# S5 scan and FFN under one gate: another order of loads and first matmuls, odd inputs seeded in PSUM

## Chip, cores, metric

One NeuronCore of one Trainium2 chip. The metric is device time in microseconds of one execution, the lower the better; for the kernel before, the median of six runs. TensorE is called PE in the profile, VectorE DVE, ScalarE ACT, GpSimd POOL, and SyncE SP; SP and ACT issue all DMAs here.

## What is computed

x has 2048 tokens of 448 columns, in bf16. A gate g weighs two branches: a diagonal complex state space layer (448 states) and an FFN (448 to 1792 to 448, silu between).

```python
g = sigmoid((x * gate_w).sum(-1, keepdims=True))
Lam_bar = exp(dt * Lam);  B_bar = ((Lam_bar - 1) / Lam)[:, None] * (B_re + 1j * B_im)
Bu = x @ B_bar.T
for t in range(L):                  # h is complex, 448 states
    h = Lam_bar * h + Bu[t]
y = 2 * (h @ (C_re + 1j * C_im).T).real + x * Dskip
out = g * y + (1 - g) * (silu(x @ w1) @ w2)
```

## The kernel before

The time axis is cut into pairs of tokens. Row k of `x2` holds tokens 2k (even, columns 0 to 447) and 2k+1 (odd); each of the two streams has 1024 positions, in halves h = 0 and 1 of 512. The scan runs over pairs: its input is Bu(odd) + lambda Bu(even), with lambda = lr + i li, its decay lambda squared; its results are the odd states, and the even ones follow from them.

**Tiles.** 448 = 3 x 128 + 64. Contractions over 448 take three steps j of 128 rows and a remainder of 64. `pair` (353) works on two banks of PSUM at once: each step is two half-row matmuls (64 rows, 512 columns), the lower half into one bank, the upper half into the other; then the remainder; and when the next pair has been started (`settle`, 334), the same main steps with the halves swapped. Of the remainder one half row lies in XT and the other in XR, a copy of 64 rows in the other partition half (`swap_xr`, 237). `late` (363) does the same with the remainder last. States are in blocks pt = 0 to 2 of 128 (real and imaginary parts in tiles m = 2pt and 2pt+1) and pt = 3, whose 64 real and 64 imaginary rows share one tile (its weights are BR, copied from BT in line 612).

**Stages.** FFN1 works on chunks c = 0, 1 (even x, h = 0, 1) and 2, 3 (odd x): 14 blocks fb of 128, silu by ACT from two banks into AT (416). FFN2 (723) makes four 128-token tiles of a chunk, 14 matmuls of 448 columns each. `bu` (757) multiplies x by B for one block and half, even and odd, and ACT copies both to SBUF: even to VE (781), odd to HS (785). `scan` on DVE: `weigh` (809) makes odd + lambda * even in three operations; `turn` rotates by tables COS and SIN and runs the real scan (834), `back` rotates back, `even` (848) makes the even states. `scan3` does pt = 3 and swaps halves by DMA. Then y (935 to 969): a tile's bank is seeded with the scaled FFN result (`yseed`) and gets seven matmuls, five in `yopen` and two (block 2) in `yclose`; `yout` scales and stores it. Block 2's scan is cut in halves and comes last.

**Order.** `Tracker` records instructions per engine in program order and puts a wait where a buffer's last writer or readers ask for it; nothing is reordered. So lines 988 to 1092 are the order written by hand, `run(g, n)` takes n steps of a generator, and `nxt` (319) deals out the eight banks in turn.

**The opening.** 26 warm-up matmuls (446) run while x and W1 load. Even x of half 0 comes as it is (XA0, XA1, XB), TensorE transposes it in blocks (`turn_x`, 450), and DVE copies these from PSUM to XT (`turned_x`, 459). All other transposed x and B come by DMA transposes on SP. `ffn1_first` (394) does steps j = 0 to 2 of six blocks at full row width. Between steps, the rows R (log_dt, Lambda, Dskip) are turned to columns (430) and a chain of small operations on DVE and ACT makes the coefficients (506 to 536); then GpSimd, DVE and ACT make the tables (`phases`, `tables`).

```python
        for j in range(2):
            turn_x(j)
            turned_x(j)
        first = ffn1_first()
        next(first)
        rd()
        T.op("pe", mm_cols, reads=["R0", "R1", "R2", "R3", "Rd", "ID"], writes=["ps7"])
```

## Time and profile before

| | |
|---|---|
| Runs | 138.76 to 139.16 us, median 139.07 (six) |
| The profiled execution | 138.98 us, its span 137.1 us |
| Busy: PE, DVE, ACT, POOL | 132.7, 121.3, 94.7, 21.7 us |
| FFN2 matmuls | 224 of 448 columns, 42.9 us |
| FFN1 half-row matmuls (XT) | 325 of 512 columns, 39.9 us |
| silu on ACT | 28, mean 1019 ns |
| DMA | 12.07 MB, mean 88 GB/s |

The page's span is the time between the first and the last recorded event on the core, the execution's own time is longer. A timeline row reads: start, length, engine, source line, operation, result <- operands, shape, count, and in brackets the idle time before the row with what ended it. Rows of matmuls overlap in their recorded lengths, so that start to start is the pace. A row of groups gives busy time, mean ns of one, and idle time before. A row of waits gives total, times and longest, in us.

### The profile page before, as it was taken

The numbers are of one execution on the slowest core, as the hardware profiler recorded it, in microseconds if no ns is written. First come the engines' busy times: TensorE is split into PE (matmuls) and PEld (weight loads), VectorE is DVE, ScalarE is ACT, GpSimd is POOL, SyncE is SP. The second block draws the span as 40 slices with busy tenths as digits, with TensorE's granted clock in tenths as the row PEclk, the third lists the DMA queues.
The fourth block names the chain that finished last, engine by engine and source line by source line (L and its number), as shares of the span: only waits on it lengthen the run. The fifth ranks groups of instructions, "written<-read, shape, count | busy, mean of one in ns | idle before, by whom it ended". The sixth has DMA issues, their size and how long they took to land.

```text
span 137.1 us, 2412 instructions
## 1 busy us (share of the span) xinstructions
PE 132.7 (97%) x959; PEld 64.9 (47%) x959; DVE 121.3 (88%) x152; ACT 94.7 (69%) x154; POOL 21.7 (16%) x32
## 2 busy tenths in 40 slices
PE   7899999999999999999999999999999999999992
PEld 7344434444434554444554444445555555555561
DVE  1379799969979999999999999999999999999663
ACT  0469799678999999799999159797124337789100
POOL 7105998406910000000000000000000000000000
PEclk9999999999999999999999999999999999999999
DMA  3999378599899220003012000000000000132124
GB/s 101 348 255 275 69 160 169 100 387 361 201 162 114 44 66 0 5 0 77 0 25 51 5 0 0 0 5 0 0 0 0 0 5 33 67 100 67 60 74 134
DMA packets 24641, 12.07 MB, mean 88 GB/s; under 512 B 16628, under 2 KB 24184, under 8 KB 24632
## 3 DMA queue, kind: packets, MB, share of 16 engines
q1 hardware_dynamic: 23044, 10.83, 32.2%
q10 hardware_dynamic: 1588, 1.11, 2.7%
q8 instruction: 7, 0.11, 0.4%
q14 instruction: 2, 0.02, 0.0%
HBM read 5.51 MB, written 1.84 MB: 54 GB/s over the span
## 4 chain that ended last, share of the span: by engine, by line
PE 78%; DVE 7%; ACT 5%; DMA 2%; POOL 2%; issue 2%; SPq 1%; ACTq 0%; DVEq 0%
PE ps L345 32%; PE ps L735 31%; PE ps L939 14%; ACT AT L416 3%; DMA R<-in_A_Lambda_re_dram 2%; ACT CO L686 2%; DVE FP L557 2%; POOL FP L550 1%; SPq L228 1%; POOL G L552 1%; DVE TMPS L963 1%; DVE BT L610 1%; DVE BR L612 1%; DVE P L500 1%; DVE P L497 1%
## 5 line engine op out<-in xcount | busy, mean ns | idle before, releaser
L735 PE MATMUL ps<-W,AT 128*128 128x448 bf16 x224 | 42.9, 353 | 0.0
L345 PE MATMUL ps<-XT,W1E 64*128 64x512 bf16 x325 | 39.9, 376 | 0.0
L735 PEld LDWEIGHTS ps<-W,AT 128*128 128x128 bf16 x224 | 21.7, 98 | 21.2 <-ACT HS L785 0.4
L416 ACT ACTIVATE AT<-ps 128x1024 bf16<-128x1024 f32 x28 | 27.9, 1019 | 4.7 <-PE ps L345 4.5
L345 PEld LDWEIGHTS ps<-XT,W1E 64*128 64x128 bf16 x325 | 16.8, 94 | 19.5 <-DVE IOTA L743 0.5
L345 PE MATMUL ps<-XT,BT 64*128 64x512 bf16 x168 | 19.9, 376 | 0.1
L748 ACT ACTIVATE BT<-ps,GT 128x448 bf16<-128x448 f32 x8 | 5.1, 633 | 13.1 <-PE ps L735 13.1
L345 PEld LDWEIGHTS ps<-XT,BT 64*128 64x128 bf16 x168 | 8.0, 94 | 10.4 <-ACT AT L416 0.6
L939 PE MATMUL ps<-CO,VE 128*128 128x448 bf16 (+1 forms) x63 | 11.6, 332 | 0.0
L939 PE MATMUL ps<-CO,HS 128*128 128x448 bf16 x56 | 11.6, 352 | 0.0
L781 ACT ACTIVATE VE<-ps 128x1024 bf16<-128x1024 f32 (+1 forms) x9 | 7.5, 834 | 5.4 <-PE ps L345 5.4
L834 DVE TENSOR_TENSOR_SCAN G<-P,Q 128x1024 f32<-128x1024 f32 (+1 forms) x6 | 11.2, 1911 | 0.0
L345 PE MATMUL ps<-XR,W1E 64*128 64x512 bf16 x25 | 9.2, 376 | 0.0
L939 PEld LDWEIGHTS ps<-CO,VE 128*128 128x128 bf16 x63 | 6.1, 98 | 4.7
L793 DVE SCALAR_TENSOR_TENSOR HS<-VE,P,G 128x512 bf16<-128x512 bf16 (+1 forms) x10 | 8.1, 856 | 0.2
L939 PEld LDWEIGHTS ps<-CO,HS 128*128 128x128 bf16 x56 | 5.5, 98 | 5.1
L785 ACT ACTIVATE HS<-ps 128x1024 bf16<-128x1024 f32 (+1 forms) x9 | 7.5, 837 | 0.0
L793 DVE SCALAR_TENSOR_TENSOR G<-VE,P,HS 128x1024 f32<-128x1024 bf16 (+1 forms) x5 | 7.5, 1490 | 0.1
L790 DVE TENSOR_TENSOR Q<-G,COS 128x2048 bf16<-128x2048 f32 (+1 forms) x4 | 7.0, 1756 | 0.1
L790 DVE TENSOR_TENSOR Q<-G,SIN 128x2048 bf16<-128x2048 f32 (+1 forms) x4 | 7.0, 1750 | 0.0
L598 DVE TENSOR_TENSOR XN<-XN,DB 128x1792 bf16<-128x1792 bf16 x4 | 4.4, 1090 | 1.3 <-DMA DB<-in_A_Dskip_dram 1.2
L790 DVE TENSOR_TENSOR Q<-Q 128x1024 bf16<-128x1024 bf16 (+1 forms) x9 | 5.2, 573 | 0.3
(118 smaller groups left out, 176.3 us busy)
## 6 DMA issues: line engine op xcount, KB each, us to landing
W<-in_B_w_dram SPq DMA_DIRECT2D x1, 1568.0 KB, 12.3
XN<-in_A_x_dram SPq DMA_DIRECT2D x1, 896.0 KB, 9.8
out_dram<-OT SPq DMA_DIRECT2D x8, 112.0 KB, 1.7
out_dram<-TMPS SPq DMA_DIRECT2D x7, 112.0 KB, 1.7
W1E<-in_B_w_dram SPq DMA_DIRECT2D x3, 224.0 KB, 4.1
HS<-HS SPq DMA_DIRECT2D x4, 128.0 KB, 2.3
W1E<-in_B_w_dram SPq DMA_DIRECT2D x1, 384.0 KB, 5.5
XN<-in_A_x_dram SPq DMA_DIRECT2D x1, 384.0 KB, 6.6
```

What stands on the lines that cost most here:

```text
L345: ins = pe.matmul(ps[:, bank, :], w(p, j), xh(odd, h, j, p), start=start and j == js[0], stop=stop and j == js[-1])
L416: T.op("act", lambda e: e.activation(a[:, fb:fb + n, :], ps[:, bank:bank + n, :], AF.Silu), reads=[f"ps{bank + i}" for i in range(n)], wri ...
L557: T.op("dve", lambda e: e.scalar_tensor_tensor(X, RR, MAGIC, X, ALU.subtract, ALU.subtract), reads=[f"F{pt}", f"G{GP[pt]}"], writes=[f"F{p ...
L598: T.op("dve", lambda e, v=v: e.tensor_tensor(v, v, DB[:, :].unsqueeze(1).to_broadcast([128, 4, D]), ALU.mult), reads=ks + ["DB"], writes=[ ...
L735: ins = pe.matmul(ps[:, bank, 0:D], a[:, fb, q * 128:(q + 1) * 128], W2[:, fb, :], start=(first and fb == 0), stop=(fb == NFB - 1), skip_g ...
L748: T.op("act", lambda e: e.activation(bs(tile), ps[:, bank, 0:D], AF.Copy, scale=sc), reads=[f"ps{bank}", "GT2" if h else "GRI"], writes=ks)
L781: T.op("act", lambda e: e.activation(VE[:, m0:m0 + n, hs], ps[:, b0:b0 + n, :], AF.Copy), reads=pe_, writes=[f"V{m}_{h}" for m in ms])
L785: T.op("act", lambda e: e.activation(HS[:, m0:m0 + n, 8 + h * 512:8 + (h + 1) * 512], ps[:, b1:b1 + n, :], AF.Copy), reads=po_, writes=[f" ...
L790: T.op("dve", lambda e: e.tensor_tensor(o, a, b, op), reads=reads, writes=writes)
L793: T.op("dve", lambda e: e.scalar_tensor_tensor(o, a, s, b, ALU.mult, ALU.add), reads=reads, writes=writes)
L834: T.op("dve", lambda e, c=c, init=init: e.tensor_tensor_scan(G[:, c, w], rb, Q1[:, c, w], init, ALU.mult, ALU.add), reads=[f"Q1{c}", "rr", ...
L939: ins = pe.matmul(ps[:, bank, c], state(kt, odd, m), CO[:, m, c], start=False, stop=(m == YB[-1]), skip_group_check=True)
```

## The change

It changes no arithmetic but that of the weighing in blocks 1 and 2, and adds no pass over data.

- **Loads.** The first x comes in four row blocks and two more column blocks, W1's first 896 columns for j = 0, 1 in two parts, alternately on SP and ACT; the rows R stand after x's first four parts. All of W1 is issued ahead of the first DMA transpose; of these, the second even half of x comes first.
- **Opening.** 22 warm-up matmuls, then two more after four transposes; step j = 0 of `ffn1_first` runs in two halves of 256 columns; transposes and copies are by half for j = 0, 1.
- **Order.** Three remainders first; three pairs of FFN1 on chunk 1 stand ahead of the first `bu`. `skip(n)` leaves out n bank numbers. The scan generators have other steps, so that DVE's order differs too.
- **Seeded odd Bu** for blocks 1 and 2: `bu_even`, then ACT copies the result to VE and writes VE times lr into the two banks into which `bu_odd` adds; `weighed` needs two operations, with an operand in PSUM. Block 2's Bu moves into FFN1 on chunk 2.
- **FFN2 on chunk 0**: no ACT seeds; DVE evacuates all four tiles.
- **XR for odd x**: two DVE copies for a DMA on ACT. `even` of block 1 uses FP instead of G.
- **y**: odd tiles first within each half, the last tile stored in parts of 280 and 168 columns instead of 224 and 224.

```diff
-NWARM = 26
+NWARM = 22
...
+        for k, eng in enumerate(("sp", "act")):
+            ld_x(eng, k)
+        ld_w("sp", 0, 0, FJ, "a")
+        ld_w("act", 0, FJ, FA, "b")
+        for k, eng in ((2, "sp"), (3, "act")):
+            ld_x(eng, k)
+        for i, (eng, v) in enumerate((("sp", A_log_dt), ("sp", A_Lambda_re), ("act", A_Lambda_im), ("act", A_Dskip))):
+            ld_row(eng, i, v)
+        ld_w("sp", 1, 0, FJ, "a")
+        ld_w("act", 1, FJ, FA, "b")
+        for i, eng in enumerate(("sp", "act")):
+            ld(eng, XH[:, 2 * i:2 * i + 2, 256:512], x0[:, 2 * i:2 * i + 2, 256:512], XA[4 + i])
+        ld("sp", W1E[0:64, 3, 0:FA], B_w1[384:448, 0:FA], "W1Ea0")
+        ld_w("act", 2)
+        T.op("act", lambda e: e.activation(JK[:, 0:1], HP[:, :], AF.Exp), reads=["HP"], writes=["JK0"])
...
+        ld_w3("sp", "W1Ee", FB, F_FF)
...
+        ldt(XT[:, 0:3, 512:1024], x2[512:1024, 0:384], "XTe1")
+        ldt(XT[:, 3:4, 512:1024], x2[512:1024, 384:512], "XTer1")
+        for i, src in enumerate((A_B_re, A_B_im)):
+            ldt(BT[:, 0:3, i * D:(i + 1) * D], src[:, 0:384], f"BT{i}")
...
-            for j in range(3):
+            for j, h in ((0, 0), (0, 1), (1, None), (2, None)):
+                c = slice(0, 512) if h is None else slice(256 * h, 256 * h + 256)
...
+                    if (j, h, fb) in ((0, 0, 3), (0, 0, 5), (1, None, 1), (1, None, 3)):
                         yield
...
+        warm(NWARM, 5)
+        PB = (6, 7, 6, 7)
...
         for j in range(2):
-            turn_x(j)
-            turned_x(j)
+            turn_x(j, 0)
+            turned_x(j, 0)
+        warm(2, 5)
         first = ffn1_first()
         next(first)
+        turn_x(0, 1)
+        turned_x(0, 1)
         rd()
+        next(first)
+        turn_x(1, 1)
+        turned_x(1, 1)
+        next(first)
...
-        ld_w3("act", "W1Ee", FB, F_FF)
...
         phases2(0)
+        swap_xr("dve", 1, 0)
         phases2(2)
         phases(3)
+        phases(1, "dve")
         T.op("dve", lambda e: e.tensor_copy(BT[0:64, 3, :], BT[64:128, 3, :]), reads=BTK[2:4],
              writes=["BTz"] + BTK[2:4])
         T.op("dve", lambda e: e.tensor_copy(
             BR[:, :, :].rearrange("p j (c n) -> p j c n", c=2),
             BT[:, :, :].rearrange("p j (c n) -> p j c n", c=2)[:, :, :, 384:448]), reads=BTK, writes=["BR"])
+        swap_xr("dve", 0, 1)
         phases2(3)
-        phases(1, "dve")
         phases2(1)
-        swap_xr("dve", 1, 0)
...
-            first = c != 2 and (c, q) not in ((0, 2), (0, 3))
+            first = c != 2
...
+            if c == 0:
                 T.op("dve", lambda e: e.scalar_tensor_tensor(
...
+        def bu_even(pt, h):
+            m, hs = 2 * pt, slice(h * 512, (h + 1) * 512)
+            b = [nxt(), nxt()]
+            vs = [f"V{m}_{h}", f"V{m + 1}_{h}"]
+
+            def done():
+                o = obank[pt, h] = [nxt(), nxt()]
+                T.op("act", lambda e: e.activation(VE[:, m:m + 2, hs], ps[:, b[0]:b[0] + 2, :], AF.Copy),
+                     reads=[f"ps{i}" for i in b], writes=vs)
+                T.op("act", lambda e: e.activation(ps[:, o[0]:o[0] + 2, :], VE[:, m:m + 2, hs], AF.Copy,
+                                                   scale=c1("lr", pt)), reads=vs + ["lr"], writes=[f"ps{i}" for i in o])
+
+            pair(*[(b[i], 0, h, lambda p, j, i=i: bt(p, j, m + i)) for i in range(2)], BTK[0:2] + XE[h][0],
+                 BTK + XE[h][0] + XE[h][1] + [f"XR{h}a"], done)
+
+        def bu_odd(pt, h):
+            m, o = 2 * pt, obank[pt, h]
+            pair(*[(o[i], 1, h, lambda p, j, i=i: bt(p, j, m + i)) for i in range(2)], BTK[0:2] + XO[h][0],
+                 BTK + XO[h][0] + XO[h][1] + [f"XR{h}b"], lambda: None, seeded=True)
...
+            def weighed(h):
+                w, o = slice(h * 512, (h + 1) * 512), obank[pt, h]
+                stt(u[:, 0, w], ve[:, 1, w], nli, ps[:, o[0], :], lk + [vk[1][h], f"ps{o[0]}"], [uk[0][h]])
+                stt(u[:, 1, w], ve[:, 0, w], li, ps[:, o[1], :], lk + [vk[0][h], f"ps{o[1]}"], [uk[1][h]])
...
-                t = TG if cut else G
-                tgk = ["F1", "CT0", "CT1"] if cut else GK
+                t, tgk = (TG, ["F1", "CT0", "CT1"]) if cut else (G, GK)
+                if pt == 1:
+                    t, tgk = FP[:, 0:2, :], ["F0", "F1", "CT0", "CT1"]
                 stt(t[:, :, :], hp[:, :, w], lr, ve[:, :, w], lk + hk + [f"HSz{pt}"] + v0[0] + v0[1], tgk)
                 stt(ve[:, 0, w], hp[:, 1, w], nli, t[:, 0, :], lk + hk + tgk, he_(a, h0, h1) + v0[0])
                 stt(ve[:, 1, w], hp[:, 0, w], li, t[:, 1, :], lk + hk + tgk, he_(b, h0, h1) + v0[1])
 
+            for h in range(2):
+                if pt:
+                    weighed(h)
+                else:
+                    weigh(h, h + 1)
+                yield
...
-        ffn1_rem(first, 0)
+        def skip(n):
+            for _ in range(n):
+                nxt()
+
+        for fb in (0, 2, 4):
+            ffn1_rem(first, fb)
         pair(*ffn1_pair(0, NF1))
-        ffn1_rem(first, 2)
-        ffn1_rem(first, 4)
-        settle()
-        for i, _ in enumerate(ffn1(0, NF1 + 2)):
-            if i:
-                run(t0, 1)
+        run(ffn1(0, NF1 + 2))
+        late([ffn1_pair(1, 0)])
+        run(t0, 1)
+        for fb in (2, 4):
+            pair(*ffn1_pair(1, fb))
+            run(t0, 1)
         bu(0, 0, late)
-        run(t0)
         bu(3, 0, late)
-        late([ffn1_pair(1, fb) for fb in (0, 2)])
+        pair(*ffn1_pair(1, 6))
         load_w2()
         bu(0, 1, split=True)
         bu(3, 1)
...
+        bu_even(1, 0)
...
+        f = ffn1(1, 8)
...
+        bu_even(1, 1)
-        T.dma("act", lambda e: e.dma_start(XR[0:64, :], XT[64:128, 7, :]), reads=XO[0][3:] + XO[1][3:],
-              writes=["XR0b", "XR1b"])
-        bu(1, 0)
+        bu_odd(1, 0)
+        run(g2, 2)
+        skip(2)
+        run(f)
+        run(g2, 2)
+        bu_odd(1, 1)
         run(g2, 3)
-        bu(1, 1)
...
         run(s0, 1)
+        run(s1, 1)
         run(g3, 1)
-        run(s0, 1)
-        for q in (2, 3):
-            ffn2_seed(q, q, 0)
-        run(t3)
+        run(s1, 1)
         ffn2(0, 0)
...
+        f = ffn1(2)
+        for i in range(4):
+            run(f, 1)
+            if i:
+                run(g2, 1)
+        bu_even(2, 0)
+        run(g2)
+        run(f, 1)
+        run(g3)
+        bu_even(2, 1)
+        run(f, 1)
+        run(t1, 1)
+        bu_odd(2, 0)
+        run(t1, 1)
+        skip(2)
+        run(f)
+        bu_odd(2, 1)
+        run(t1)
+        settle()
...
-        bu(2, 1)
-        run(s2, 4)
...
-        tiles = [(0, 1), (1, 1), (0, 0), (2, 1), (1, 0), (3, 1), (2, 0), (3, 0)]
+        tiles = [(kt, 1) for kt in range(4)] + [(kt, 0) for kt in range(4)]
...
-        while opened:
+        for n in range(1, 8):
             ahead()
             yout(*yclose(*opened.pop(0)))
-            if len(seeds) > 1 or tiles:
+            if n in (2, 3, 4, 6):
...
-        for c in (slice(0, D // 2), slice(D // 2, D)):
+        for c in (slice(0, 280), slice(280, D)):
```

## The prediction

> **What bounds the kernel now.** I read the page first (engine shares, chain), then the timeline of TensorE, where every gap shows, then the waits, and last the groups of ScalarE and VectorE that the change touches.
>
> ```profile
> span 137.1 us, 2412 instructions
> PE 132.7 (97%) x959; PEld 64.9 (47%) x959; DVE 121.3 (88%) x152; ACT 94.7 (69%) x154; POOL 21.7 (16%) x32
> PE 78%; DVE 7%; ACT 5%; DMA 2%; POOL 2%; issue 2%; SPq 1%; ACTq 0%; DVEq 0%
> ```
>
> TensorE is the bound: busy for 97% of the span, and 78% of the chain. So time is won only where TensorE stands still or starts late, and the next thing to read is its timeline.
>
> ```profile
> 0.82 2.88 PE L442 MATMUL ps<-const-bfloat16-1.0 128*128 128x128 bf16 x26 [0.82 <-PEq L1113]
> 3.65 0.69 PE L455 MATMUL ps<-ID,XN 128*128 128x128 bf16 x8
> 4.71 1.46 PE L398 MATMUL ps<-XT,W1E 128*128 128x512 bf16 x6 [0.38 <-DVE XT L460]
> 6.37 0.24 PE L433 MATMUL ps<-ID,R 128*128 128x4 bf16 x4 [0.20 <-DVE R L427]
> ...
> 17.07 2.11 PE L345 MATMUL ps<-XT,BT 64*128 64x512 bf16 x18
> 19.43 0.82 PE L345 MATMUL ps<-XT,BR 64*128 64x512 bf16 x6 [0.26 <-DVE BR L612]
> ...
> 30.67 1.67 PE L345 MATMUL ps<-XT,W1E 64*128 64x512 bf16 x13
> 31.97 0.38 PE L345 MATMUL ps<-XR,W1E 64*128 64x512 bf16 x1
> 32.18 1.67 PE L345 MATMUL ps<-XT,W1E 64*128 64x512 bf16 x13
> ```
>
> Rows overlap, since a matmul's recorded end lies past the next one's start; starts are what count. From 30.67 to 32.18 fourteen half-row matmuls start, seven pairs: 0.216 us a pair, the pace of one 512-column matmul too. Against that pace: six from 4.71 end at 6.00, but the next starts at 6.37 (0.37 lost, to the parameter rows R); eighteen half rows from 17.07 end at 19.01, the next starts at 19.43 (0.42 lost, to the copy BR). Start to start, the trace holds three smaller losses: 0.12 before the third step of the first FFN1 (8.34), 0.28 at 39.16, 0.15 at 56.16. FFN2 and y run at 0.19 a matmul without a hole. The rest of the idle time is the opening: nothing useful but eight transposes before 4.71.
>
> ```profile
> DVE R L427 <- DMA R<-in_A_Lambda_re_dram: 1.2, 1, 1.2
> PEld ps L398 <- DMA W1E<-in_B_w_dram: 0.5, 1, 0.5
> PEld ps L345 <- DVE IOTA L743: 0.5, 1, 0.5
> PE ps L345 <- DVE BR L612: 0.3, 1, 0.3
> ```
>
> These waits name the causes: the row loads, W1, a drained FFN2 bank, the BR copy.
>
> **What the Trainium skill says.** "TensorE: Matmul & The Clock Gate", section "What's actually happening": the array runs at half clock until a free-running activity window of about 3.4 us was busy. The trace agrees: 0.107 us a warm-up matmul, full clock from 3.50. Its "Back-to-back issue gap" gives N/2.4 + 2.5 ns: 109 ns for 256 columns (no row here shows that size), 216 for 512, as measured. "ScalarE: Activation LUTs", section "What ACT_TABLE_LOAD costs": 186 ns plus 0.833 ns per column, 93 more for a per-partition scale, 93 of overlap. For 1024 columns with a scale that is an estimate of 1.13, one each 1.04; the rows without such a scale measure 1.02. "DMA: Bandwidth & Descriptors", section "Issuing engines are not separate DMA queues": both queues share the same 16 engines, so splitting W1 over two saves issue time, and only the order of bytes matters. The trace agrees: 348 GB/s in the slice 3.4 to 6.9 us, whichever queue the bytes came from.
>
> **Step 1, the opening.** Before the first FFN1 the old order must land 256 KB of x and 224 KB of W1 (x at 3.60 and 3.78, the first W1 block at 4.45 by the landing events). The new one needs the first two row blocks of x (128 KB) and 96 KB of W1. 128 KB less at 348 KB/us is 0.37 us: x at 3.25 to 3.35, W1's parts at 3.9 to 4.1. TensorE: 22 warm-ups end at 0.82 + 22 x 0.107 = 3.18; two transposes at 3.35, a VectorE copy of 128x256 (the 128x512 one takes 0.42, so 0.28), with 0.17 of drain: first FFN1 at 4.0, not 4.71. But only four transposes are done, not eight: 4 x 0.056 = 0.22 is still owed. First-half matmuls (six of 0.109) and four transposes end at 4.87, the second half's copy comes at 5.05: a new stall of about 0.2. Splitting step 0 costs 12 x 0.109 against 6 x 0.216: nothing.
> The rows R now stand behind 480 KB, not 960: 480/348 = 1.4 us earlier, 4.7 to 4.9. They are needed at 6.1, so the 0.37 goes. What is late next is W1's third block. It stands behind the same 1296 KB as before, lands at 7.1 to 7.5 and is needed at 7.55, where the copied j=2 tile arrives too. So step j=2 starts at 7.55 instead of 8.34, with the same work behind it: **0.79 won**.
>
> **Step 2, into silu.** Six matmuls of j=2, then three remainder steps, then a pair: banks 0 and 1 are wanted again at 10.4. ScalarE's first silu waits for Exp and Sin links of the coefficient chain, which start earlier, and should begin at 9.6 (10.31 before) and end at 10.55. **0.15 lost**; bounds 0 and 0.4.
>
> **Step 3, order of loads.** All transposes stand behind W1 (2080 KB, landed near 9.2 to 9.6), so B's transposes lose to x's second even block. That block is wanted near 15.1 and should land by 11 to 12; B's first is wanted at 19.6, and should land by 15; odd x by 16. I take no cost, since three FFN1 pairs (4.5 us) now stand ahead of Bu; cover gone means a wait one for one beyond some 3.5 us of lateness. BR's copy ends near 20.3 and is wanted after 22: **0.42 won**.
>
> The queues: SP now issues ten loads ahead of its first transpose, some 5.2 instead of 3.78, hidden since bytes run out later (9.2). ScalarE issues eight ahead of the Exp table load, which moves from 3.34 to 4.7 and ends at 6.2 with its first use; the first Exp waits for R's columns until 6.6 anyway. If that cover of 0.4 is gone, the delay goes into step 2. The last W1 part leaves ScalarE's queue at 7.45 (0.40 of issue), and the XR DMA at 36.13 (0.50) gives way to VectorE copies.
>
> **Step 4, seeded odd Bu.** Per block and half the old path evacuates even and odd by ScalarE (1.02 each), then VectorE does three operations; the new one writes lr times the even result into the odd banks (1.1) and VectorE does two:
>
> ```profile
> L793 DVE SCALAR_TENSOR_TENSOR HS<-VE,P,G 128x512 bf16<-128x512 bf16 x8 | 5.7, 749 | 0.1
> L793 DVE SCALAR_TENSOR_TENSOR G<-VE,P,HS 128x1024 f32<-128x1024 bf16 x4 | 5.1, 1276 | 0.1
> L785 ACT ACTIVATE HS<-ps 128x1024 bf16<-128x1024 f32 x5 | 5.1, 1021 | 0.0
> L963 DVE SCALAR_TENSOR_TENSOR OT<-ps,GT,BT 128x448 bf16<-128x448 f32 x4 | 2.7, 682 | 1.9 <-PE ps L939 1.9
> ```
>
> An operand in PSUM costs VectorE 0.68 for 448 columns, so 0.75 for 512, the same as from SBUF. Old VectorE work: 2.35 + 2 x 1.28 for block 1 and 4 x 0.75 + 2 x 1.28 for block 2; new 4 x 0.75 each. It saves 4.4 us, gives back 2 x 0.67 for two FFN2 tiles that move over from ScalarE and 2 x 0.29 for XR copies: 2.5 net. None of it is on TensorE's path, so it counts zero; it is slack. The cost is PSUM: even results and seeds hold four banks until ScalarE has run 1.02 + 1.1 in series behind a silu; the skipped bank numbers shift which bank waits for whom, and add no instruction. A seeded bank is free only when VectorE has reached its `weighed`. The hole of 0.28 at 39.16 is of this kind, and I expect its like (0.27) near 38 and 0.1 near 65. The 0.15 at 56.16 is a VectorE read of FFN2 and goes if VectorE is not late: **0.05 won**. Bounds: 0.2 won to 1.2 lost.
>
> **Step 5, y and the end.** With odd tiles first, VectorE's scan of block 2 (ends 127.16 now) need not be earlier; TensorE has no hole in y today and gets none. The last part shrinks from 224 to 168 columns: 0.44 becomes 0.39 behind the last matmul, **0.05 won**.
>
> **Sum.** 0.79 - 0.15 + 0.42 + 0.05 + 0.05 = 1.16. The profiled execution took 138.98 (span 137.1 and 1.9 around it), 0.09 under the median of six, 139.07. 138.98 - 1.16 = 137.8.
>
> **Rivals.** (a) The parts land no sooner: 512-byte rows and fixed latency hold x at 3.6 and W1 at 4.4. For it: a landing lags its last packet by 0.5 us; against it: bytes pace the rest. Then 0.37 + 0.42 - 0.2 and 0.1 remain: 138.3. (b) Banks: each of the four seeded halves makes TensorE wait 0.3. For it: 69% ScalarE, and a hole there already; against it: 6 to 7 us of FFN1 lies between. 1.2 lost: 139.0. (c) The clock: with an idle 0.2 at 3.2 and 0.3 at 3.6 the window is missed, and 3.4 us more run at half clock; 1.7 lost less 0.5 of idle that absorbs it: 139.0. Against it: the old opening had 0.6 idle at 4.1 and kept its clock. (d) Slower: all four tiles of the first FFN2 are now read by VectorE in its queue among scans, and its scan of block 3 waits for the half-swap DMA, queued behind W2 (1568 KB). VectorE may be 1 us late at 53 before FFN1's banks are missing; from there each us goes to TensorE. A swap that lands 3 us late loses 2: 139.8. Against it: the 2.5 us VectorE saves.
>
> **How the numbers follow.** Main case 0.67 (137.0 to 138.4), (a) 0.13, (b) 0.08, (c) 0.04, (d) 0.08. About 0.2% is what a measurement tells from no change. Faster: main and (a), 0.80; same: (b) and (c), 0.12; slower: (d), 0.08. The range 137.0 to 138.9 leaves out (d), most of (b) and (c), and a little below.
>
> **What would show it.** First FFN1 matmul at 4.0 and j=2 near 7.55; no wait on R or BR; ScalarE waits of TensorE near 10.5, 38 and 65 under 0.4; none on VectorE near 55; full clock by 3.6; y without a hole. Wrong if a bank wait over 0.5 us, or a wait on a transposed load, appears after 15 us.

## The result and the profile after

139.53 us, the median of 20 runs (138.87 to 140.00), against 139.06 for the kernel before in the same comparison: a ratio of 1.0032, with a 95% interval of 1.0020 to 1.0044. The change makes the kernel slower by 0.3%. The profiled execution took 139.80 us.

The page of the changed kernel, span, busy times and chain:

```profile
span 137.7 us, 2426 instructions
...
PE 133.0 (97%) x963; PEld 66.2 (48%) x963; DVE 119.0 (86%) x157; ACT 93.4 (68%) x150; POOL 17.9 (13%) x32
...
PE 92%; ACT 3%; DVE 2%; issue 0%; DVEq 0%
```

TensorE now holds 92% of the chain, where it held 78%. That looks like a better kernel. But a span that is 0.6 us longer has come with 0.3 us more of PE busy time, so the rest is standing still, and the timeline says where. TensorE's opening, and Bu's last block, in the changed kernel:

```profile
4.02 1.01 PE L411 MATMUL ps<-XT,W1E 128*128 128x256 bf16 x4
4.82 0.42 PE L471 MATMUL ps<-ID,XN 128*128 128x128 bf16 x2
5.04 0.55 PE L411 MATMUL ps<-XT,W1E 128*128 128x256 bf16 x2
5.42 0.28 PE L471 MATMUL ps<-ID,XN 128*128 128x128 bf16 x2
5.63 1.26 PE L411 MATMUL ps<-XT,W1E 128*128 128x256 bf16 x8
6.72 0.24 PE L450 MATMUL ps<-ID,R 128*128 128x4 bf16 x4
...
7.70 0.59 PE L411 MATMUL ps<-XT,W1E 128*128 128x512 bf16 x2
9.51 1.47 PE L411 MATMUL ps<-XT,W1E 128*128 128x512 bf16 x6 [1.22 <-DVE P L521]
...
24.74 0.82 PE L357 MATMUL ps<-XT,BR 64*128 64x512 bf16 x6
```

Read it in this order. The first FFN1 starts at 4.02, as forecast. The row for R (6.72) has no bracket any more, and neither has the one for BR (24.74): both waits are gone. Two transposes take 0.42 us at 4.82 and 0.28 at 5.42: the array went over to full clock between them. The trace's clock record says at 5.38; before, it was 3.50. And step j = 2, which started at 8.34 before and was forecast for 7.55, starts at 9.51, behind a hole. The bracket names a small VectorE operation, which ended just then. The list of waits has the other half, TensorE's weight loads (PEld) ahead of its matmuls:

```profile
PEld ps L411 <- DMA W1E<-in_B_w_dram: 2.0, 2, 1.7
...
PE ps L411 <- DVE P L521: 1.2, 1, 1.2
```

The weight load waits for the DMA of W1, 1.7 us at a stretch. By the landing events W1's third block is there at 9.47 (at 7.55 before). VectorE's operation has nothing to do with it; it is merely the last event before the start.

How fast did the loads run? The windows view of the kernel before gives, for each microsecond, busy time of PE, PEld, DVE, ACT, POOL, the granted clock, the DMA engines' busy share and GB/s, which over 1 us is KB:

```profile
3.00:4.00 1.00, 1.00 (x13) 0.78 (x11) 0.00 (x0) 0.66 (x1) 0.83 (x4) 1.00 1.10 367
4.00:5.00 1.00, 0.62 (x8) 0.35 (x6) 0.76 (x2) 0.82 (x2) 0.13 (x2) 1.00 1.13 377
5.00:6.00 1.00, 1.00 (x6) 0.32 (x4) 0.00 (x0) 0.00 (x0) 0.00 (x0) 1.00 1.07 378
```

The same view of the changed kernel:

```profile
3.00:4.00 1.00, 0.97 (x10) 0.65 (x8) 0.42 (x2) 0.00 (x0) 0.83 (x4) 1.00 0.87 244
4.00:5.00 1.00, 0.98 (x6) 0.74 (x7) 0.08 (x1) 0.56 (x1) 0.13 (x2) 1.00 0.90 231
5.00:6.00 1.00, 1.00 (x11) 0.77 (x9) 0.63 (x3) 0.93 (x2) 0.00 (x0) 1.00 1.06 289
```

1122 KB moved in these three microseconds before, 764 after, 358 KB less. A little of that had come sooner: from 2 to 3 us the changed kernel had moved 239 KB against 166. (PEclk is 1.00 throughout; this column shows the throttle's grant, not the half clock of the opening, which is seen in the pace of the matmuls.)

### The profile page after: what moved, and what is told of

Its sections match the earlier page's. It is cut to its first block, busy times and chain, and to the rows that moved or that the text cites. A ratio compares the mean times of both kernels' runs of the same rounds, so it can differ in the third digit from the quotient of the medians.

```text
span 137.7 us, 2426 instructions
## 1 busy us (share of the span) xinstructions
PE 133.0 (97%) x963; PEld 66.2 (48%) x963; DVE 119.0 (86%) x157; ACT 93.4 (68%) x150; POOL 17.9 (13%) x32
## 4 chain that ended last, share of the span: by engine, by line
PE 92%; ACT 3%; DVE 2%; issue 0%; DVEq 0%
PE ps L357 40%; PE ps L761 31%; PE ps L1000 15%; PE ps L411 3%; PE ps L459 2%; ACT VE L824 1%; ACT ps L826 1%; ACT AT L433 1%; DVE TMPS L1024 1%; PE ps L425 1%; PE ps L471 1%; DVE XT L477 0%; ACT CO L712 0%; DVE XR L540 0%; DVE W1E L500 0%
## 5 line engine op out<-in xcount | busy, mean ns | idle before, releaser
L357 PE MATMUL ps<-XT,W1E 64*128 64x512 bf16 x325 | 40.4, 376 | 0.1
L433 ACT ACTIVATE AT<-ps 128x1024 bf16<-128x1024 f32 x28 | 28.1, 1018 | 9.3 <-PE ps L357 8.4
L357 PE MATMUL ps<-XT,BT 64*128 64x512 bf16 x160 | 20.6, 376 | 0.0
L887 DVE TENSOR_TENSOR_SCAN G<-P,Q 128x1024 f32<-128x1024 f32 (+1 forms) x6 | 11.4, 1920 | 0.0
L1000 PE MATMUL ps<-CO,VE 128*128 128x448 bf16 (+2 forms) x63 | 11.1, 332 | 0.0
L1000 PE MATMUL ps<-CO,HS 128*128 128x448 bf16 x56 | 11.1, 352 | 0.0
L841 DVE SCALAR_TENSOR_TENSOR VE<-HS,P,FP 128x512 bf16<-128x512 bf16 (+1 forms) x7 | 6.6, 977 | 0.1
L411 PE MATMUL ps<-XT,W1E 128*128 128x256 bf16 (+1 forms) x24 | 5.4, 357 | 1.3 <-DVE P L521 1.2
L841 DVE SCALAR_TENSOR_TENSOR FP<-HS,P,VE 128x1024 f32<-128x1024 bf16 (+1 forms) x4 | 6.2, 1550 | 0.1
L841 DVE SCALAR_TENSOR_TENSOR HS<-VE,P,ps 128x512 bf16<-128x512 bf16 x8 | 5.5, 735 | 0.0
L992 ACT ACTIVATE ps<-XN 128x448 f32<-128x448 bf16 x9 | 4.6, 538 | 1.0 <-DVE OT L1024 1.0
```

The costliest lines, as they stand in the source:

```text
L357: ins = pe.matmul(ps[:, bank, :], w(p, j), xh(odd, h, j, p), start=start and j == js[0], stop=stop and j == js[-1], skip_group_check=seeded)
L411: T.op("pe", lambda pe, fb=fb, bank=bank, j=j, h=h, c=c: pe.matmul(ps[:, bank, c], W1E[:, j, fb * 128:(fb + 1) * 128], XT[:, j, c], start= ...
L433: T.op("act", lambda e: e.activation(a[:, fb:fb + n, :], ps[:, bank:bank + n, :], AF.Silu), reads=[f"ps{bank + i}" for i in range(n)], wri ...
L841: T.op("dve", lambda e: e.scalar_tensor_tensor(o, a, s, b, ALU.mult, ALU.add), reads=reads, writes=writes)
L887: T.op("dve", lambda e: e.tensor_tensor_scan(G[:, c, w], rb, Q1[:, c, w], init, ALU.mult, ALU.add), reads=[f"Q1{c}", "rr", f"G{c}"], write ...
L992: T.op("act", lambda e: e.activation(ps[:, bank, 0:D], s, AF.Copy), reads=[f"BS{tile}" if kt < 4 else f"XD{block(tile)}"], writes=[f"ps{ba ...
```

## The experiments

Theory A was that the new order of loads across the two queues lets SP's later parts of W1 pass the third block; the first expectations name its rivals. Later ones were formed as runs fell: I (too many loads to issue), O (order alone), C (TensorE's clock), L (late loads), H (the rows R leave the queues dry), S (the smaller loads themselves). Ratios are against the kernel before, run beside them.

**First batch: which part of the change costs?**

e1_w2_on_sp: the third block changes queues with the first remainder.

```diff
-        ld("sp", W1E[0:64, 3, 0:FA], B_w1[384:448, 0:FA], "W1Ea0")
-        ld_w("act", 2)
+        ld("act", W1E[0:64, 3, 0:FA], B_w1[384:448, 0:FA], "W1Ea0")
+        ld_w("sp", 2)
```

> The changed kernel with one exchange: W1's third block goes to SP's queue ahead of the later parts of W1, its 64-row remainder to ScalarE's queue in its place. Theory A (order): the third block came late because it stood on ScalarE's queue, where SP's later parts (448 KB of them by 9.25 us) share the engines with it. Then it lands near 7.5, step j=2 starts near 8.1, and the time falls by 1.4 us to about 138.1. Theory B (rate): more and smaller transfers on two queues cut the load rate from 373 to 250 GB/s. Then the third block lands at 8.3 or later, and the time is 138.7 or more.

Measured: 139.43 us, 1.0016 (1.0001 to 1.0031). The block lands at 7.95 and the hole ahead of j = 2 is gone, but the timeline of this version shows another:

```profile
7.59 2.00 PE L411 MATMUL ps<-XT,W1E 128*128 128x512 bf16 x8
...
11.00 1.03 PE L357 MATMUL ps<-XT,W1E 64*128 64x512 bf16 x7 [0.65 <-DMA W1E<-in_B_w_dram]
```

The second remainder of W1 (64 rows) now lands at 10.77 and TensorE waits 0.65 for that. Theory A had the right wait and the wrong price: the medians are 0.1 apart and their intervals overlap, so no gain in time can be told.

e2_w1_whole: W1's blocks 0 and 1 in one load each instead of two parts.

```diff
-        ld_w("sp", 0, 0, FJ, "a")
-        ld_w("act", 0, FJ, FA, "b")
+        ld_whole("sp", 0)
...
-        ld_w("sp", 1, 0, FJ, "a")
-        ld_w("act", 1, FJ, FA, "b")
+        ld_whole("act", 1)
```

> The changed kernel with W1's first two blocks each in one transfer, block 0 on SP and block 1 on ScalarE, the third where the change put it. Theory A (order): the third block still lands near 9.2 and the time stays within 0.3 us of the changed kernel's 139.5. Theory B (rate): the rate in 3.5 to 8.2 us goes up towards 350 GB/s, the third block lands by 8, time about 138.3.

Measured: 139.88 us, 1.0067 (1.0041 to 1.0094); the block lands at 9.89. Fewer loads of W1 do not help by themselves.

e3_old_opening: loads of x, R and W1 (the second later part late on ScalarE again), warm-ups, transposes and `ffn1_first` as in the kernel before; the order of all that follows, seeding and y as changed.

```diff
-NWARM = 22
+NWARM = 26
-        XA = ["XA0", "XA1", "XA2", "XA3", "XB0", "XB1"]
+        XA = ["XA0", "XA1", "XB"]
...
-            for j, h in ((0, 0), (0, 1), (1, None), (2, None)):
+            for j in range(3):
```

> The changed kernel with the opening of the kernel before (its loads up to W1's last part, 26 warm-ups, whole transposes and copies, whole step j=0); the order of the DMA transposes and all that follows stay as changed. Both theories: j=2 at 8.3 as before; the wait on BR (0.42) is gone and so is most of the first wait on silu, so 138.4. If it is 139.0 or more, something after the opening eats the gain and the third block is not the whole cause.

Measured: 138.79 us, 0.9984 (0.9974 to 0.9994). This splits the change: all but the opening gains 0.3 us, and the new opening loses 139.53 - 138.79 = 0.74. Its timeline:

```profile
4.79 1.79 PE L397 MATMUL ps<-XT,W1E 128*128 128x512 bf16 x6 [0.18 <-DMA W1E<-in_B_w_dram]
6.79 0.24 PE L432 MATMUL ps<-ID,R 128*128 128x4 bf16 x4 [0.21 <-DVE R L426]
...
8.20 2.01 PE L397 MATMUL ps<-XT,W1E 128*128 128x512 bf16 x8
```

Full clock came at 5.49 here, as late as in the changed kernel, so the clock is not what sets the two profiles apart. The last two matmuls of j = 1 start at 8.20 and 8.41, j = 2 at 8.75, with the block there since 8.16: no wait, and 0.76 sooner than 9.51. That agrees with the 0.74 of the medians.

e4_w2_split: the third block in two parts, one a queue, ahead of the first remainder.

```diff
+        ld_w("sp", 2, 0, FJ, "a")
+        ld_w("act", 2, FJ, FA, "b")
         ld("sp", W1E[0:64, 3, 0:FA], B_w1[384:448, 0:FA], "W1Ea0")
-        ld_w("act", 2)
```

> The changed kernel with W1's third block in two parts on both queues, as blocks 0 and 1, ahead of everything that is wanted later. Theory A (order): it lands near 7.5 as in the exchange of queues, time about 138.1. Theory B (rate): one more transfer, so no better than 138.9.

Measured: 139.19 us, 1.0010 (0.9993 to 1.0027), landings 7.64 and 8.56. Half of the loss is back, in the median; the profiled execution, 138.67, was the fastest of 22, so its profile is not typical.

**Second batch: is it the number of loads to issue?**

f1_x_two_loads: the first half-columns of x in two loads.

```diff
-        for k, eng in enumerate(("sp", "act")):
-            ld_x(eng, k)
+        for i, eng in enumerate(("sp", "act")):
+            T.dma(eng, lambda e, i=i: e.dma_start(XH[:, 2 * i:2 * i + 2, 0:256], x0[:, 2 * i:2 * i + 2, 0:256]),
+                  writes=XA[2 * i:2 * i + 2])
...
-        for k, eng in ((2, "sp"), (3, "act")):
-            ld_x(eng, k)
```

> The changed kernel, with the first half-columns of x in two loads (one a queue, two row blocks each, as in the kernel before) and all else as changed. One load less stands ahead of W1's third block on ScalarE's queue; a load took 0.41 to 0.46 us of its issuer in the trace of the changed kernel, and the bytes stay the same. Theory I (the opening is short of issued loads: 945 of the 960 KB issued by 3.7 us had moved by 5.7): the third block is issued at 3.5 instead of 3.93 and lands by 9.0 or sooner; 139.2 us. Theory O (only the order of bytes counts, the later parts on SP's queue overtake the block however early it is issued): lands at 9.3 to 9.5; 139.5 us. Theory C (the clock): 139.5 us, spread unchanged.

Measured: 139.58 us, 1.0022 (1.0008 to 1.0036). The block is issued at 3.65 and lands at 8.99. That is within what the changed kernel shows itself (9.47 and, below, 8.95), but also what theory I had forecast (9.0 or sooner), so the landing decides nothing. The time speaks against I, which had forecast 139.2; but x comes later here, so that the first FFN1 starts at 4.50 instead of 4.02, and this loss can hide a small gain.

f2_rows_gpsimd: the rows R issued by GpSimd, in the changed kernel. f4_old_rows_gpsimd: the same edit in the version of e3.

```diff
-(("sp", A_log_dt), ("sp", A_Lambda_re), ("act", A_Lambda_im), ("act", A_Dskip))
+(("pool", A_log_dt), ("pool", A_Lambda_re), ("pool", A_Lambda_im), ("pool", A_Dskip))
```

> The changed kernel, with the four row loads of R issued by GpSimd in place of SP and ScalarE; nothing else moves. They cost SP 0.56 us and ScalarE 0.78 us of issue time in the trace of the changed kernel and carry under 4 KB. Theory I (issue): the second block's parts are issued at 2.2 to 2.3 and the third block at 3.15 instead of 3.93; it lands near 8.3 and TensorE's wait of 1.38 us ahead of step j=2 falls to 0.4 or so; 138.9 us. Theory O: tiny loads move no bytes out of the way, so the block still lands past 9.2; 139.5 us. Theory C: 139.5 us.

> The version with the old opening and the new order behind it (138.79 us), with the four row loads of R issued by GpSimd. Theory I: the third block is issued at 2.35 instead of 2.92 and lands up to 0.5 us sooner unless the 16 engines pace it (the old opening moved 345 GB/s from 3.5 to 5.7 us); the rows come sooner too, so TensorE's wait of 0.21 us for them goes; 138.5 us. Theory O: only the rows' wait goes, 138.7 us. Theory C: 138.8 us.

Measured: 141.38 us, 1.0155 (1.0136 to 1.0174), and 142.67 us, 1.0234 (1.0206 to 1.0262). Bad experiments for their question: GpSimd builds the identity for the transposes, and its issuing comes first, so TensorE stands there. What they show is the price of standing early and of a late clock. f4's timeline:

```profile
4.39 1.01 PE L454 MATMUL ps<-ID,XN 128*128 128x128 bf16 x8 [0.64 <-POOL ID L304]
5.58 2.72 PE L397 MATMUL ps<-XT,W1E 128*128 128x512 bf16 x6 [0.18 <-DVE XT L459]
9.72 0.25 PE L432 MATMUL ps<-ID,R 128*128 128x4 bf16 x4 [1.42 <-DVE R L426]
...
11.91 2.40 PE L397 MATMUL ps<-XT,W1E 128*128 128x512 bf16 x9
```

Six matmuls take 2.7 us (0.43 each, half clock), and the clock record gives full clock only at 12.49. f4 takes 3.9 us more than e3. The two idle stretches, 0.64 and 1.42, are 2.06 of that; most of the rest lies in the half clock that lasts 7 us longer (5.49 in e3). One thing bears on theory I all the same: in f2 the third block is issued at 3.17 instead of 3.93 and still lands at 9.48.

f3_four_more_rows: four more row loads ahead of W1, in the version of e3.

```diff
+        for i, (eng, v) in enumerate((("sp", A_log_dt), ("sp", A_Lambda_re), ("act", A_Lambda_im), ("act", A_Dskip))):
+            ld(eng, GWB[i:i + 1, 0:D], row(v), f"JR{i}")
+        ld("act", XH[:, :, 256:512], x0[:, :, 256:512], "XB")
         ld_w("sp", 0)
```

> The version with the old opening and the new order behind it (138.79 us in its own run), with four more row loads, two a queue, put behind the first loads of x and ahead of all of W1; they write a tile that is not read before it is loaded again, and carry under 4 KB. Theory I: W1's first block is issued 0.55 us later and so is everything behind it; the first FFN1 at about 5.3, the third block near 8.7; 139.25 us. Theory O and theory C: no bytes to speak of, so nothing moves; 138.8 us.

Measured: 140.65 us, 1.0084 (1.0056 to 1.0113), four times the forecast loss. W1's first block is issued 0.67 later than in e3 (1.97 against 1.30) and lands 1.02 later (5.72); TensorE stands 1.17 us for it, misses its clock (full at 9.68), and the rest follows. Loads with almost no bytes are not free ahead of the first weights.

**Third batch: order made strict, and second profiles.**

g1_split_later_parts_last: e4 with W1's later parts on ScalarE's queue, behind the second remainder. g4_old_later_part_last: the same for the one later part in the version of e3.

```diff
-        ld_w3("sp", "W1Ed", FA, FB)
         ld("act", W1E[0:64, 3, FA:], B_w1[384:448, FA:], "W1Ea1")
-        ld_w3("sp", "W1Ee", FB, F_FF)
+        ld_w3("act", "W1Ed", FA, FB)
+        ld_w3("act", "W1Ee", FB, F_FF)
```

> The version with the third block in two parts on both queues (139.19 us in its run), with the later parts of W1 (columns 896 on) moved from SP's queue to ScalarE's, behind the last remainder load. Nothing that is wanted later can overtake what is wanted first. Theory L (late loads: the third block, then the 64-row remainders, set the opening): the third block by 8.0, the remainders by 8.6 and 9.1, no wait on a load from TensorE; 138.6 us. Theory C (TensorE itself, at half clock until a release that comes at 3.5 in one execution and at 5 to 7 in others, sets the opening): the loads come sooner and nothing is won; 139.2 us with a spread of over 1 us.

> The version with the old opening and the new order behind it (138.79 us), with the first later part of W1 moved from SP's queue to ScalarE's, behind both remainder loads. Theory L: the third block lands by 7.7 instead of 8.16 and the second remainder by 8.7 instead of 9.55; 138.5 us. Theory C: TensorE reaches step j=2 at 8.7 by its own pace, so only the small wait for the second remainder (0.1 to 0.3) goes; 138.6 to 138.8 us.

Measured: 144.88 us, 1.0390 (1.0349 to 1.0431), and 139.91 us, 1.0062 (1.0039 to 1.0085). The opposite of theory L's forecast. With its loads moved away, SP comes to its DMA transposes sooner, at 4.80 instead of 5.96 in g1 and at 3.32 instead of 3.80 in g4, while ScalarE's queue still has loads outstanding. The windows view of g1:

```profile
5.70:8.20 2.50, 2.42 (x25) 1.70 (x24) 0.93 (x5) 0.67 (x4) 0.00 (x0) 1.00 1.24 255
8.20:10.70 2.50, 1.33 (x7) 0.37 (x6) 1.16 (x4) 1.50 (x3) 0.00 (x0) 1.00 1.00 61
```

61 GB/s for 2.5 us, with the DMA engines shown as busy. The longest of TensorE's waits for W1 in g1, in its timeline:

```profile
15.43 0.82 PE L358 MATMUL ps<-XT,W1E 64*128 64x512 bf16 x6 [3.42 <-DMA W1E<-in_B_w_dram]
```

After standing that long, TensorE fell back to half clock from 16.24 to 19.66, so the 144.88 has a second part. In g4 the third block landed early (7.17), but TensorE stood 0.68 us for the last part of W1, which landed at 11.77. Both versions that let transposes start while ScalarE had loads outstanding lost time. But that such an overlap stops loads is not a rule: in the kernel before, ScalarE's last part of W1, 288 KB issued at 7.45 and landed at 12.30, shares its time with SP's transposes (issued from 3.78 on, landing from 10.09 on), and the windows view shows full flow.

```profile
10.00:11.00 1.00, 1.00 (x12) 0.40 (x10) 0.90 (x7) 0.89 (x2) 0.00 (x0) 1.00 1.23 320
11.00:12.00 1.00, 1.00 (x12) 0.48 (x10) 0.90 (x7) 1.00 (x2) 0.32 (x1) 1.00 1.21 305
```

What makes the difference is not known.

g2_after_again and g3_before_again: both kernels unchanged, for a second profile each.

> The changed kernel once more, for a second profile. Theory L: the third block lands at 9.2 to 9.7 again and step j=2 starts behind it, whatever the clock. Theory C: full clock from another time than 5.38 (anything from 3.5 to 7), and the start of j=2 moves with it only if it comes after 7.

> The kernel before once more, for a second profile: was the full clock from 3.50 us, on which the forecast's timing of the opening rests, typical? Theory C: another time, 4.5 to 6.9, and step j=2 starts later than 8.34 by about half of the difference (8.7 to 9.2), in an execution that takes within 0.5 us of 139.1 all the same. Theory L: j=2 waits for the third block near 8.3 whatever the clock.

Measured: 139.52 us and 138.94 us. The changed kernel, this time in an execution that is its median:

```profile
8.21 0.59 PE L411 MATMUL ps<-XT,W1E 128*128 128x512 bf16 x2
8.99 1.47 PE L411 MATMUL ps<-XT,W1E 128*128 128x512 bf16 x6 [0.18 <-DVE XT L477]
```

The block lands at 8.95 and j = 2 starts at 8.99. By its own pace TensorE would have been there at 8.21 + 2 x 0.216 = 8.64 (full clock at 6.6, by the spacing of its matmuls). So both count: with the block in time it would start 0.35 sooner; with full clock in time but the block as late, no sooner at all. The kernel before had full clock at 3.49 again; theory C's forecast of 4.5 to 6.9 for it was wrong, and that the clock of this very kernel varies is not shown.

**Fourth batch: the order of late loads, in both openings.**

h1_split_again: e4 once more, for a typical profile. h3_split_remainder_first: e4 with the second remainder on SP ahead of the later parts. h4_old_remainder_first: the same move in the version of e3.

```diff
+        ld("sp", W1E[0:64, 3, FA:], B_w1[384:448, FA:], "W1Ea1")
         ld_w3("sp", "W1Ed", FA, FB)
-        ld("act", W1E[0:64, 3, FA:], B_w1[384:448, FA:], "W1Ea1")
```

> The version with the third block in two parts on both queues once more, for a second profile (the first one, 138.67 us, was the fastest of its 22 executions; the median is 139.19). Theory L (late loads set the opening): an execution near 139.2 shows a wait on a load of W1 (third block or remainders) of 0.4 us or more that the first did not have. Theory C (TensorE's own pace at half clock): it shows no such wait, but full clock from 6.3 us or later instead of 5.54.

> The split version (139.19 us) with the second remainder load moved from ScalarE's queue to SP's, ahead of the two later parts, so that the later parts stand behind it on one queue and the transposes still come last. Theory L: the remainder lands by 9.0, no wait on it, and the spread of over 1 us narrows; 138.7 us. Theory C: 139.1 to 139.2 us, the spread stays.

> The version with the old opening and the new order behind it (138.79 us) with the second remainder load moved to SP's queue, ahead of the later part. Theory L: it lands by 9.0 instead of 9.55, and the 0.1 to 0.3 us that TensorE stands before it go; 138.6 us. Theory C: 138.8 us.

Measured: h1 139.02 us (one execution), with a wait of 0.31 us for the second remainder, which lands at 9.87 (9.49 in e4), in spite of full clock at 4.47: for theory L, though it had forecast 0.4 or more. h3 138.87 us, 0.9980 (0.9968 to 0.9993), spread 138.51 to 139.49. Its timeline:

```profile
7.53 2.15 PE L412 MATMUL ps<-XT,W1E 128*128 128x512 bf16 x8
...
10.60 1.03 PE L358 MATMUL ps<-XT,W1E 64*128 64x512 bf16 x7
```

No row of FFN1 shows a bracket here, but a bracket tells of an engine that was idle, and in this stretch recorded lengths overlap. The list of waits from 5 to 11 us shows weight loads that still wait:

```profile
PEld ps L412 <- DMA W1E<-in_B_w_dram: 1.0, 3, 0.5
...
PEld ps L358 <- DMA W1E<-in_B_w_dram: 0.6, 1, 0.6
```

j = 2 starts at 8.08, where TensorE's own pace gives 7.96 (the same 0.12 is lost in the kernel before, where no load is late); its fourth matmul starts 0.14 late, behind the block's second part, which landed at 8.81; some 0.2 each is lost ahead of the two remainders (9.13 and 9.71). So the late loads are sooner than in the changed kernel, not all in time. A block in two parts and late loads in a good order win 0.66 of the 0.74 us; of that, by the medians, the split alone (e4) accounts for about half. Full clock came at 3.91 in this profile, so what the order is worth rests on the medians. h3 is faster than both kernels, as e3 is; between h3 and e3 (0.08 apart, intervals overlapping) there is no difference to be told.

h4: 139.25 us, 1.0016 (1.0003 to 1.0029). Slower than e3, though its loads land sooner (third block 7.19, second remainder 7.79) and its span is the shortest of all, 136.8 us. The loss is not inside the span: over 22 executions each, the median span is 136.8 us here and 136.9 in e3, and the time outside it 2.4 us against 1.9. Neither theory had forecast that, and what fills that time no run shows.

h5_before_swap_alone: in the kernel before, the third block and the first remainder change queues, and nothing else.

```diff
-        ld_w("sp", 2)
+        ld("sp", W1E[0:64, 3, 0:FA], B_w1[384:448, 0:FA], "W1Ea0")
...
-        ld("act", W1E[0:64, 3, 0:FA], B_w1[384:448, 0:FA], "W1Ea0")
+        ld_w("act", 2)
```

> The kernel before with one thing of the change alone: W1's third block (224 KB) and the first remainder (112 KB) change places, so that the block is issued by ScalarE and SP's first later part can move beside it. Issue time and bytes stay as they were. Theory L: the block lands at 8.2 to 8.8 instead of 7.2 to 7.6, TensorE waits for it; 139.5 us. Theory C: TensorE reaches that step at 8.3 or later anyway, so 139.1 to 139.2 us.

Measured: 139.18 us, 1.0013 (0.9994 to 1.0032): no change. The block lands at 7.55, just as on SP. So the other queue did no harm in this test, where loads ran at 376 KB a microsecond from 4 to 5 us. It took the slow loads of the new opening to make the order cost anything.

**Last: what makes the loads slow?** From 4 to 5 us the windows view shows 358 to 383 GB/s in all seven profiles whose opening loads are those of the kernel before (f3, with more rows ahead, apart), and 121 to 231 in all that have the new ones, e2 (140) and f1 (147) among them. The rows R, which now stand behind 480 KB instead of 960, were the suspect left.

k1_rows_later: the changed kernel with the rows behind x's second half-columns. k2_best_rows_later: the same move in h3.

```diff
-        for i, (eng, v) in enumerate((("sp", A_log_dt), ("sp", A_Lambda_re), ("act", A_Lambda_im), ("act", A_Dskip))):
-            ld_row(eng, i, v)
         ld_w("sp", 1, 0, FJ, "a")
...
             ld(eng, XH[:, 2 * i:2 * i + 2, 256:512], x0[:, 2 * i:2 * i + 2, 256:512], XA[4 + i])
+        for i, (eng, v) in enumerate((("sp", A_log_dt), ("sp", A_Lambda_re), ("act", A_Lambda_im), ("act", A_Dskip))):
+            ld_row(eng, i, v)
```

> The changed kernel (139.53 us) with the four row loads of R issued behind x's second half-columns instead of ahead of W1's second block, so behind 960 KB as in the kernel before; issue times of the third block and of all that follows stay as they were. Theory H (the rows take both issuers for 0.6 to 0.8 us while only 480 KB are under way, and the loads run dry): from 4 to 5 us at least 300 KB move instead of 160 to 220, the second block lands by 5.5, the third by 8.4, the rows near 6.2, in time for TensorE at 6.7; 139.0 us. Theory S (the smaller loads themselves are slow): the hole stays, third block past 8.9; 139.5 us.

> The version with the third block on both queues and both remainders ahead of the later parts (138.87 us), with the same move of the four row loads. Theory H: the third block by 8.0, the remainders by 8.5 and 9.1, so that TensorE waits for no load after its first step; 138.6 us, faster than both kernels. Theory S: 138.9 us.

Measured: 140.45 us, 1.0107 (1.0064 to 1.0151), and 141.92 us, 1.0180 (1.0139 to 1.0221). Theory H falls, at least as the whole cause: k1's window is as empty as ever, although its third block landed at 8.51, nearer to H's forecast of 8.4 than to S's of past 8.9.

```profile
4.00:5.00 1.00, 0.98 (x6) 0.74 (x7) 0.08 (x1) 0.52 (x1) 0.13 (x2) 1.00 0.72 134
```

And the move made a new wait that I had overlooked, in k1's list of waits:

```profile
DVE R L444 <- DMA R<-in_A_Dskip_dram: 1.6, 1, 1.6
...
PE ps L411 <- DVE XT L477: 0.9, 1, 0.9
```

In VectorE's queue `rd` stands ahead of the copy of x that step j = 1 needs. The rows land at 6.9 to 7.1, VectorE waits 1.6 us for them, TensorE 0.9 us for VectorE; in k2, where they land at 8.3 to 8.5, it is 2.46 us, and after that TensorE is at half clock again from 9.42 to 12.83. So neither time is a price of the loads alone.

## Why the prediction was wrong, point by point

**The step that failed** is in step 1: "What is late next is W1's third block. It stands behind the same 1296 KB as before, lands at 7.1 to 7.5 and is needed at 7.55". The bytes ahead are right, the times are not. It landed at 9.47 and 8.95, and TensorE itself came at 8.14 and 8.64, not 7.55. The forecast of 0.79 won became 9.51 - 8.34 = 1.17 lost in the first profile. Of the error of 1.96, TensorE's own lateness is 8.14 - 7.55 = 0.59 and the late block 9.51 - 8.14 = 1.37; in the second profile it is 1.09 and 0.35. In medians, which is what the kernel paid, the new opening lost 0.74 where 0.79 had been forecast as won.

**The term of the block** came from 348 KB a microsecond, a rate that the old loads had reached, applied to new ones. These ran at 121 to 231 from 4 to 5 us. And the block is not alone on the way: by 9.25 us some 440 KB of SP's later parts had moved with it. The Trainium skill, "DMA: Bandwidth & Descriptors", section "Issuing engines are not separate DMA queues", says that DMAs of different issuers "interleave with each other". The traces agree, by these 440 KB. I drew from it that only the order of bytes matters, but counted only the bytes issued ahead of the block; those issued behind it on the other queue shared the way. The runs show what each part costs. The queue swapped at the old rate costs nothing (h5). With the slow loads in a good order the kernel ends as soon as with the old opening (h3 against e3); but TensorE started FFN1 0.77 sooner there (4.02 against 4.79), so slow loads and clock still cost that head start. The bad order on top of them costs 0.66 to 0.74. That much is shown. Which property of the new loads makes them slow is not: the rows' place (k1), x in four loads (f1) and W1 in parts (e2) were each undone alone, and the hole stayed. All undone together is e3, without the hole. Not tried were pairs of them, x's later columns in one load, and another rival: how much is issued early. By 2.25 us 960 KB have been issued in the kernel before and in e3, but 480 KB in the changed kernel, and about as little in f1, e2, f2 and k1; about as much (505 KB) had moved by 4.0 us in the changed kernel, when its flow fell. None of these versions puts the bytes back.

**The term of the clock.** "Full clock from 3.50" was read as a fact of the kernel. The Trainium skill, "TensorE: Matmul & The Clock Gate", section "What's actually happening", says that the window is free-running and that the same kernel differs from run to run. The runs agree only across versions: leaving out those that make TensorE stand early (f2, f3, f4), the clock records give 3.49 to 6.6 us, and two profiles of the changed kernel 5.38 and about 6.6; but both profiles of the kernel before give 3.50 and 3.49. Whether the change itself moves the clock is open, since versions with the new opening's loads have 3.91 too, and versions with the old one's 6.52. What a late clock cost can be read: a 256-column matmul took 0.213 us at half clock and 0.109 after, and all of TensorE's 0.59 arises between 4.02 and 5.63, while from there to j = 2 it would have needed 2.51 (forecast 2.50). So the opening's gain was too high by 0.6 to 1.1 us even with every load in time. Rival (c) named this, for idle gaps; no gap was needed.

**Right in step 1:** first FFN1 at 4.02 (forecast 4.0), rows at 4.45 to 4.62 in the first profile (4.7 to 4.9), no wait for R.

**Step 2:** the 0.15 for the first silu was not lost; TensorE, late itself, waits for no bank at 10.5. But the forecast that silu begins at 9.6 was wrong. ScalarE in the changed kernel:

```profile
10.11 0.30 ACT L527 ACTIVATE P<-P,HP 128x4 f32<-128x4 f32 x1 [0.20 <-DVE P L524]
11.35 1.02 ACT L433 ACTIVATE AT<-ps 128x1024 bf16<-128x1024 f32 x1 [0.94 <-PE ps L425]
```

The last link of the coefficient chain (L527) ends at 10.41, just as in the kernel before, although the rows came 1.3 us earlier; here silu (L433) waits on TensorE. In h3, where TensorE is sooner, silu starts right behind this link at 10.58, and TensorE's weight load waits for its bank:

```profile
11.63 0.54 PEld L358 LDWEIGHTS ps<-XT,W1E 64*128 64x128 bf16 x7 [0.49 <-ACT AT L434]
```

In no profile here does the chain end before 10.31. An estimate from these figures: with every load on time but the chain no sooner, banks wanted at 10.4 would come free near 11.4, a silu of 1.02 after the chain's end. That is a loss of up to 1.0 instead of 0.15, so much of the 0.79 might not have shown even then.

**Step 3:** the 0.42 for BR is won, and TensorE waits for no transposed load after 15 us. But these loads landed later than forecast (the second even half at 13.39 and 14.30 instead of 11 to 12, odd x at up to 26.46 instead of 16), and VectorE does wait for two of them:

```profile
22.13 0.39 DVE L637 COPY BT<-BT 64x896 bf16<-64x896 bf16 x1 [1.29 <-DMA BT<-in_A_B_im_dram]
...
23.42 0.29 DVE L240 COPY XR<-XT 64x512 bf16<-64x512 bf16 x1 [0.47 <-DMA XT<-in_A_x_dram]
```

That is one of the signs of being wrong that were named, and it cost nothing here: BR's copy ends at 22.94 (20.3 forecast), and TensorE wants it at 24.74. So the loads are covered, with less to spare than reckoned.

**Step 4:** the prices held, and VectorE is busy 2.3 us less (2.5 forecast). Groups of the changed kernel:

```profile
L841 DVE SCALAR_TENSOR_TENSOR HS<-VE,P,ps 128x512 bf16<-128x512 bf16 x8 | 5.5, 735 | 0.0
...
L826 ACT ACTIVATE ps<-VE,P 128x1024 f32<-128x1024 bf16 x4 | 4.5, 1118 | 0.1
```

0.735 for an operand in PSUM (forecast 0.75), 1.12 for the seed (1.1). The holes are 0.31 at 39.95 and 0.15 at 67.53 (forecast 0.27 and 0.1), none near 55.

**Step 5** and y: no hole; from the last matmul's start to the end of the span it takes 2.71 us instead of 2.91, 0.20 won (0.05 forecast). In sum, the steps after the opening gave what was forecast: j = 2 starts 1.17 later while the span grows by 0.6, so some 0.6 comes back (forecast 0.42 + 0.05 + 0.05 - 0.15 = 0.37); in medians, e3 gains 0.3. The sum also took 1.9 us around the span as fixed; it is 2.1 in both profiles of the changed kernel, another 0.2 that no step had.

**Rivals.** (b), waits on banks in the seeded halves, did not happen beyond the 0.31 at 39.95, where the kernel before lost 0.28. (a), parts that land no sooner, is nearest, but it feared for x and W1's first block, which came in time; the loads behind them were late. The rival that ended slower, (d), did so by a mechanism that no run shows; that its number is near the measured one is luck.

## What to carry to other kernels

A rate of loads belongs to those loads: before moving bytes in time, check how many are under way at each microsecond in the new order, and give each block that is waited for a place that nothing on the other queue can share. The clock of one profile need not be that of the next version; cost an opening at half clock as well. And when a small load is moved, look in the queue of whoever consumes it for what stands behind.

## What the hardware showed unexpectedly

- With DMA transposes issued from 4.80 us on while ScalarE's loads were outstanding, the flow fell from 255 to 61 GB/s for 2.5 us (g1). The kernel before overlaps such loads too, at 320 and 305. What decides it stays open.
- Where the record has both ends, full clock lasts 133.12 us from its start in every profile with a span of up to 138.2 us, and 129.71 in f3 and f4: 39 and 38 times 3.413 us, the window that the Trainium skill gives ("TensorE: Matmul & The Clock Gate", section "What's actually happening"). On that grid a first window with 79% of TensorE busy was enough (before: 0.82 idle up to its start, full at 3.50); windows with some 70% (the changed kernel's second profile) and with 76 to 77% (f4, twice) were not. By these figures, as an estimate, some 0.8 us of idle time in one window can cost another 3.4 us of half clock.
- The time outside the span is not constant: in medians over the executions, 1.9 us before, 2.05 after, 2.4 in h4. Its cause stays open.
